# Folded x rounded to bf16 in one step, tables over all 256 features, weights loaded into freed buffers: what each part does to the time

## Chip, cores, metric

The kernel runs on one core of a Trainium2 chip. The metric is the time of one execution in microseconds of the device (us), as the median of several executions. "Ratio" always means the mean time of one kernel's fast runs over the mean time of the fast runs of the kernel before in the same rounds on the same chip, so it is not quite the ratio of the medians that are quoted beside it. A run that the record marks as slow (over 1.5% above the fastest of its kernel) is left out of the ratios. Engines: TensorE (PE in the profile, PEld its weight loads), VectorE (DVE), ScalarE (ACT), GpSimd (POOL), SyncE (SP).

## The reference

A Fourier mixing of x (8 x 2496 x 256, the real part of a transform over both axes) is followed by a mixture of 8 experts with balanced assignment: all (token, expert) logits are sorted, and each token goes to the first expert in that order which is not yet full.

```python
X = np.fft.fft(np.fft.fft(x, axis=1), axis=2).real        # (8, 2496, 256) -> 19968 tokens
logits = x @ w_gate                                        # 256 -> 8 experts
order = np.argsort(-logits.flatten())                      # greedy, capacity N // E per expert
for idx in order: ...                                      # first free expert wins
for e in range(E):
    out[assigned == e] = np.maximum(x[assigned == e] @ w1[e], 0) @ w2[e]   # 256 -> 1024 -> 256
```

The kernel does not sort the logits. It assigns most tokens in a first round ("early" tokens, 40 tiles), starts the experts on them, and settles the rest beside them ("settling": small VectorE steps with joins to TensorE). The tokens settled last form 16 "late" tiles, whose rows are gathered by index.

## The kernel before

Five stages follow each other: (1) fold x along both axes and project it on the gate, (2) logits, (3) first assignment, Fourier transforms, sorting of rows into expert tiles, (4) expert tiles with settling beside them, (5) the tail. The last cut is made in both kernels where tile 25 is put, that is, where its rows are scattered to the output by index: there the changed kernel gathers its first late rows, while the kernel before does so at tile 28. Names in the profiles: zt are transposed rows of x, hps and hb the hidden values of a tile before and after the ReLU, ops and ot its outputs, wps and w1t a turned w1, xg gathered late rows. The parts that the argument touches:

```python
# stage 1, per batch b of 8: fold to fp32 z, round z on ScalarE, transpose z
nc.vector.tensor_tensor(a_t[:, :, :, 1:D], a_t[:, :, :, 1:D], b_t[:, :, ::-1, D - 1:0:-1], op=AL.add)
nc.vector.tensor_tensor(a_t[:, :, :, 0], a_t[:, :, :, 0], b_t[:, :, ::-1, 0], op=AL.add)
z = early.tile([P, 2 * NK, D], FT, tag="z", bufs=2, name="z")
nc.vector.tensor_tensor(z[:, :, 1:P], pv[:, :, 1:P], pv[:, :, D - 1:P:-1], op=AL.add)
nc.vector.tensor_tensor(z[:, :, P + 1:D], pv[:, :, 1:P], pv[:, :, D - 1:P:-1], op=AL.subtract)
nc.scalar.copy(zball[:, b], z)
# ... transposes tp of z, copies zt <- tp on ScalarE, matmuls yps <- zt ...

# stage 3: one after the other
run(choose(True)); finish_round = raise_first(first_strips)      # assignment chain on VectorE
for n in range(4 * NT): transform(n)                             # TensorE
# ... four turn_w (w1 turned into the transformed basis), then the sorts ...

# stages 4 and 5: between parts of a tile, settling steps are taken from a generator
G0 = 28                                      # tile at which the first late gather is issued
def place_all():                             # whatever is left of the settling, at once
    if not placed: placed.append(len(list(todo)))
def pace():
    credit[0] = min(credit[0] + 1.4, 1.4)    # credit in us of VectorE work, per third of a tile
    while credit[0] > 0.0:
        c = next(todo, "end")
        if c is SYNC: return                 # a join: the rest waits for the next call
        credit[0] -= c
```

Of the kernel before, what the change touches and what calls it, by code (L numbers as in the profile page):

```python
# [8 lines left out]
FT = mybir.dt.float32  # L9
# [9 lines left out]
B = 8  # L19
S = 2496  # L20
# [33 lines left out]
KC = 64  # L54
SYNC = None
# [11 lines left out]
def kernel(  # L67
# [15 lines left out]

    tabs_cm = tc.tile_pool(name="tabs", bufs=1, side="right")
# [10 lines left out]
    for b in range(B):  # L95
        for i in range(NK):
            nc.gpsimd.iota(mir_i[:, b * NK + i:b * NK + i + 1], pattern=[[0, 1]],
                           base=(b + 1) * (S // 2) - 1 - (1 + i * P), channel_multiplier=-1)
    x_pairs = x.rearrange("b (s r) d -> (b s) (r d)", r=2)

    def load_x(b):
        a_t = early.tile([P, NK, 2, D], FT, tag="xa", bufs=2, name="xa")
        b_t = early.tile([P, NK, 2, D], FT, tag="xb", bufs=2, name="xb")
# [28 lines left out]
    kgrid_i = early.tile([P, KP], FT, tag="prod", bufs=1, name="kgrid_i").bitcast(I32)  # L132
# [60 lines left out]
    mt_f = early.tile([P, 2, D], FT, name="mt_f")  # L193
    mt_b = const.tile([P, 2, D], BF, name="mt_b")

    def phases(dst_r, kk, row, period):
        kw = dst_r.shape[-1]
        prod = early.tile([P, KP], FT, tag="prod", bufs=1, name="prod")[:, :kw]
        rnd = early.tile([P, KP], FT, tag="rnd", bufs=1, name="rnd")[:, :kw]
        nc.vector.tensor_scalar(prod, in0=kk, scalar1=row, scalar2=None, op0=AL.mult)  # L200
        nc.scalar.activation(rnd, prod, ACT.Copy, bias=0.0, scale=1.0 / period)
        nc.vector.tensor_scalar(rnd, in0=rnd, scalar1=MAGIC, scalar2=MAGIC, op0=AL.add, op1=AL.subtract)
        nc.vector.scalar_tensor_tensor(dst_r, in0=rnd, scalar=-float(period), in1=prod, op0=AL.mult, op1=AL.add)

    for dc in range(2):
        row = early.tile([P, 1], FT, tag="drow", bufs=2, name="drow")
        nc.vector.tensor_scalar(row, in0=iota_p, scalar1=float(dc * P), scalar2=None, op0=AL.add)
        r_t = early.tile([P, KP], FT, tag="rt", bufs=1, name="rt")[:, 0:P + 1]
        phases(r_t, kgrid[:, 0:P + 1], row, D)
        ra = early.tile([P, KP], FT, tag="ra", bufs=1, name="ra")[:, 0:P + 1]  # L210
        nc.vector.scalar_tensor_tensor(ra, in0=r_t, scalar=-1.0, in1=r_t, op0=AL.mult, op1=AL.max)
        nc.scalar.activation(mt_f[:, dc, 0:P + 1], ra, ACT.Sin, bias=halfpi, scale=-2.0 * PI / D)
        nc.scalar.activation(mt_f[:, dc, P + 1:D], r_t[:, 1:P], ACT.Sin, bias=0.0, scale=-2.0 * PI / D)
    nc.vector.tensor_copy(mt_b, mt_f)
# [3 lines left out]
    nc.vector.memset(g_sb, 0.0)  # L218
    gps = psl.tile([P, 512], FT, tag="tp", bufs=4, name="gps")
    for j in range(2):  # L220
        for dc in range(2):
            nc.tensor.matmul(gps[:, j * E:(j + 1) * E], lhsT=mt_f[:, dc, j * P:(j + 1) * P],
                             rhs=wg_sb[:, dc, :], start=(j == 0 and dc == 0), stop=(j == 1 and dc == 1))
    nc.vector.tensor_copy(g_sb[:, 0, 0:E], gps[:, 0:E])
    nc.vector.tensor_scalar(g_sb[:, 1, 0:E], in0=gps[:, E:2 * E], scalar1=is0, scalar2=None, op0=AL.mult)
    nc.vector.tensor_scalar(g_sb[:, 1, E:2 * E], in0=gps[:, E:2 * E], scalar1=not0, scalar2=None, op0=AL.mult)
# [5 lines left out]
    def gen_tab(i, r):  # L232
        period = S // 2 if r == 0 else S
        row = early.tile([P, 1], FT, tag="drow", bufs=2, name="drow")
        nc.vector.tensor_scalar(row, in0=m_cols[:, i:i + 1], scalar1=1.0 if r == 0 else 2.0,
                                scalar2=float(r), op0=AL.mult, op1=AL.add)
        r_t = early.tile([P, KP], FT, tag="rt", bufs=1, name="rt")
        phases(r_t, kgrid, row, period)
        ra = early.tile([P, KP], FT, tag="ra", bufs=1, name="ra")
        nc.vector.scalar_tensor_tensor(ra, in0=r_t, scalar=-1.0, in1=r_t, op0=AL.mult, op1=AL.max)  # L240
        n = "EO"[r]
        for nm, src, bias, scale in (("c" + n, ra, halfpi, -2.0 * PI / period), ("s" + n, r_t, 0.0, 2.0 * PI / period)):
            tf = early.tile([P, KP], FT, tag="tf", bufs=1, name="tf")
            nc.scalar.activation(tf, src, ACT.Sin, bias=bias, scale=scale)  # L244
            if i == NK - 1 and nm != "sE":
                nc.vector.tensor_scalar(tf, in0=tf, scalar1=own if nm == "cE" else skip, scalar2=None, op0=AL.mult)
            nc.scalar.copy(hi[nm][:, i, :], tf)
            nc.vector.tensor_tensor(lo[nm][:, i, :], tf, hi[nm][:, i, :], op=AL.subtract)


    zball = tabs.tile([P, B, 2 * NK, D], BF, name="zball")
# [6 lines left out]
    for b in range(B):  # L258
# [4 lines left out]
        z = early.tile([P, 2 * NK, D], FT, tag="z", bufs=2, name="z")  # L263
        nc.vector.tensor_tensor(z[:, :, 1:P], pv[:, :, 1:P], pv[:, :, D - 1:P:-1], op=AL.add)
        nc.vector.tensor_tensor(z[:, :, P + 1:D], pv[:, :, 1:P], pv[:, :, D - 1:P:-1], op=AL.subtract)
        nc.scalar.copy(z[:, :, 0:D:P], pv[:, :, 0:D:P])
        if b + 2 < B:
            load_x(b + 2)
        nc.scalar.copy(zball[:, b], z)  # L269


# [4 lines left out]
        for n0, nn in ((0, 4), (4, 4), (8, 2)):  # L276
            yps = psl.tile([P, 4, P], FT, tag="y", bufs=2, name="yps")
            for blk in range(2):
                tp = psl.tile([P, 4, P], FT, tag="tp", bufs=4, name="tp")
                for u in range(nn):  # L280
                    nc.tensor.transpose(tp[:, u, :], z[:, n0 + u, blk * P:(blk + 1) * P], identf)  # L281
                zt = early.tile([P, 4, P], FT, tag="zt", bufs=2, name="zt")
                nc.scalar.copy(zt[:, 0:nn, :], tp[:, 0:nn, :])  # L283
                nc.tensor.matmul(yps[pb:pb + 2 * E, 0:nn, :], lhsT=g_sb[:, blk, :], rhs=zt[:, 0:nn, :],  # L284
                                 start=(blk == 0), stop=(blk == 1))
            nc.scalar.copy(yt[pb:pb + 2 * E, n0:n0 + nn, :], yps[pb:pb + 2 * E, 0:nn, :])  # L286

        if b % 4 == 3:
            for n0, nn in ((0, 4), (4, 4), (8, 2)):
                ytp = psl.tile([P, 4, P], FT, tag="tp", bufs=4, name="ytp")  # L290
# [12 lines left out]
    ps_cm.__exit__(None, None, None)  # L303


    asg_c = ctx.enter_context(tc.tile_pool(name="asg_c", bufs=1, side="left"))
    lg = asg_c.tile([P, E, GC], FT, name="lg")
    with tc.tile_pool(name="pslog", bufs=1, space=PS) as pslog:
# [14 lines left out]
        pool6 = early.tile([P, 2 * NK, D], FT, tag="z", bufs=2, name="pool6").rearrange("p a d -> p (a d)")  # L323
        t6 = [pool6[:, q * 320:(q + 1) * 320].rearrange("p (k f) -> p k f", k=NK) for q in range(6)]
# [59 lines left out]
    mv = asg.tile([P, GC], FT, name="mv")  # L384
    mvv = mv.rearrange("p (b q k) -> p b q k", b=B, q=4)
    nc.gpsimd.memset(mv, -1.0e9)  # L386
    tail0 = asg.tile([P, 1], FT, name="tail0")
    tail1 = asg.tile([P, 1], FT, name="tail1")
    head1 = asg.tile([P, 1], FT, name="head1")
    nc.gpsimd.tensor_scalar(tail0, in0=iota_p, scalar1=113.0, scalar2=2.0e9, op0=AL.is_ge, op1=AL.mult)  # L390
    nc.gpsimd.tensor_scalar(tail1, in0=iota_p, scalar1=112.0, scalar2=2.0e9, op0=AL.is_ge, op1=AL.mult)
    nc.gpsimd.tensor_scalar(head1, in0=is0, scalar1=2.0e9, scalar2=None, op0=AL.mult)
    for q in range(4):
        nc.gpsimd.tensor_scalar(mvv[:, :, q, NK - 1], in0=mvv[:, :, q, NK - 1],
                                scalar1=tail0 if q < 2 else tail1, scalar2=None, op0=AL.add)
        if q % 2 == 1:
            nc.gpsimd.tensor_scalar(mvv[:, :, q, 0], in0=mvv[:, :, q, 0], scalar1=head1, scalar2=None, op0=AL.add)


    base = asg.tile([P, E, GC], BF, name="base")  # L400
    for e in range(E):
        nc.gpsimd.memset(base[:, e, :], float(2 * e * SEG))
# [16 lines left out]
    rampw_i = asg.tile([P, EW + 2], I32, name="rampw_i")  # L419
# [5 lines left out]

    def payloads():
        pay_i = rampw_i[:, 0:GC]
        nc.gpsimd.iota(rampw_i, pattern=[[1, EW + 2]], base=1, channel_multiplier=0)
        nc.gpsimd.tensor_copy(rampw, rampw_i)
        for q, (s1, s2) in enumerate(((0, 1), (2, -1), (1, -1), (1, 1))):  # L430
            for par in range(2):
                nc.gpsimd.iota(pay_i.rearrange("p (n k b q) -> p n k b q", n=4, k=NK, b=2)[:, :, :, par, q],
                               pattern=[[2 * S, 4], [s2 * P, NK]], base=PAY0 + S // 2 * s1 + par * S,
                               channel_multiplier=s2)
# [27 lines left out]
    def choose(first):  # L462
# [20 lines left out]
        for e in range(E):  # L483
            nc.scalar.activation(cjunk, dd[:, e, :], ACT.Relu, bias=1.0, scale=K_CNT, accum_out=cnt[:, e:e + 1])  # L484
            busy["A"] += 0.33
            if e % 4 == 3:
                yield 0.3
# [699 lines left out]
```

## Time and profile before

Three timed runs before the change: median 702.12 us (696.42 to 705.18). The profile of the kernel before that came with them spans only 658.9 us. First the page's line of busy times, then the view of busy time by stretch; each row of that is a stage.

```profile
PE 517.7 (79%) x4003; PEld 359.7 (55%) x4003; DVE 428.8 (65%) x1062; ACT 362.5 (55%) x842; POOL 318.1 (48%) x399
```

```profile
core 0: us, PE busy (x) PEld busy (x) DVE busy (x) ACT busy (x) POOL busy (x), PEclk, DMA share, GB/s
0.00:138.90 138.90, 81.70 (x285) 30.37 (x286) 92.04 (x167) 90.47 (x153) 59.12 (x88) 0.87 0.50 152
138.90:153.00 14.10, 12.96 (x316) 12.65 (x317) 8.75 (x15) 4.75 (x8) 0.00 (x0) 0.82 0.02 4
153.00:249.30 96.30, 67.65 (x536) 51.02 (x534) 63.16 (x155) 40.40 (x107) 39.80 (x93) 0.91 0.91 224
249.30:432.20 182.90, 169.99 (x1367) 124.12 (x1364) 140.89 (x418) 134.33 (x367) 77.45 (x74) 0.97 0.29 91
432.20:659.00 226.80, 185.38 (x1509) 141.54 (x1506) 123.98 (x309) 92.57 (x208) 141.69 (x145) 0.91 0.21 67
```

No engine is full in stage 1 and 3 (TensorE 82 of 139 and 68 of 96 us); in stage 4 TensorE is (170 of 183). In stage 1 the page's group of gate matmuls shows what TensorE waits for: 28.6 us idle before them, 28.4 of it for the ScalarE copies zt.

```profile
L284 PE MATMUL yps<-zt,g_sb 128*16 128x512 f32 (+1 forms) x96 | 50.7, 636 | 28.6 <-ACT zt L283 28.4
```

In the tail, the waits between 440 and 490 us (engine, line, what it waited for: us in all, times, longest) show a hole: the settling left over at tile 28 runs alone, while GpSimd waits 25.2 us for its result before it can gather, ScalarE 26.3 us for the next hidden matmul, and TensorE serves the chain in short bursts (19.26 us busy of the 40 from 440 to 480).

```profile
ACT hb L860 <- PE hps L1036: 27.7, 5, 26.3
POOL xg L1012 <- DVE wa L671: 25.2, 1, 25.2
PE inv_ps L649 <- DVE o_eq L645: 19.1, 8, 10.4
```

### The profile page before, as it was taken

The numbers are of one execution on the slowest core, as the hardware profiler recorded it, in microseconds if no ns is written. First come the engines' busy times: TensorE is split into PE (matmuls) and PEld (weight loads), VectorE is DVE, ScalarE is ACT, GpSimd is POOL, SyncE is SP. The second block draws the span as 40 slices with busy tenths as digits, with TensorE's granted clock in tenths as the row PEclk, the third lists the DMA queues.
The fourth block names the chain that finished last, engine by engine and source line by source line (L and its number), as shares of the span: only waits on it lengthen the run. The fifth ranks groups of instructions, "written<-read, shape, count | busy, mean of one in ns | idle before, by whom it ended". The sixth has DMA issues, their size and how long they took to land.

```text
span 658.9 us, 11484 instructions
## 1 busy us (share of the span) xinstructions
PE 517.7 (79%) x4003; PEld 359.7 (55%) x4003; DVE 428.8 (65%) x1062; ACT 362.5 (55%) x842; POOL 318.1 (48%) x399
## 2 busy tenths in 40 slices
PE   0675697666688659989979999894399999887894
PEld 0321232265467435657757777673377777665673
DVE  3887694368785457868858878768875555433451
ACT  1478776764145446767767867753055455333451
POOL 8786410006433411534524444433067777777774
PEclk9979867879789998999989999997589999989898
DMA  8778440003996784422222323221012222222221
GB/s 257 220 238 265 145 151 1 0 2 46 239 268 247 233 246 107 118 70 90 98 69 96 116 91 103 88 80 39 0 55 80 82 78 87 72 66 67 78 83 56
DMA packets 35169, 74.63 MB, mean 113 GB/s; under 512 B 6115, under 2 KB 14349, under 8 KB 35104
## 3 DMA queue, kind: packets, MB, share of 16 engines
q0 software_dynamic: 23296, 42.10, 24.5%
q1 hardware_dynamic: 11808, 31.73, 14.1%
q8 instruction: 33, 0.54, 0.4%
q14 instruction: 32, 0.26, 0.1%
HBM read 51.26 MB, written 32.24 MB: 127 GB/s over the span
## 4 chain that ended last, share of the span: by engine, by line
PE 55%; DVE 13%; ACT 12%; DMA 9%; POOL 5%; issue 4%; POOLq 0%; DVEq 0%; ACTq 0%; SPq 0%
PE hps L1036 18%; PE ops L1047 17%; PE yps L284 6%; PE fftps L882 3%; PE sps L960 3%; DMA out_dram<-ot,rows_l 3%; ACT zball L269 3%; ACT cjunk L484 2%; DMA t_dram<-stage 2%; PE tp L281 2%; POOL xg L1012 1%; DMA w1raw<-in_moe_w_dram 1%; ACT tf L244 1%; ACT yt L286 1%; DMA xl<-t_dram 1%
## 5 line engine op out<-in xcount | busy, mean ns | idle before, releaser
L1047 PE MATMUL ops<-w2t,hb 128*128 128x256 bf16 (+1 forms) x1344 | 177.6, 276 | 11.0 <-ACT ot L860 11.0
L1051 POOL DMA_INDIRECT out_dram<-ot,rid x120 | 124.2, 1035 | 121.1 <-ACT ot L860 78.0
L860 ACT ACTIVATE hb<-hps 128x384 bf16<-128x384 f32 (+1 forms) x293 | 131.1, 490 | 74.0 <-PE hps L1036 68.5
L1047 PEld LDWEIGHTS <-hb 128*128 128x128 bf16 (+1 forms) x1344 | 134.2, 100 | 46.3 <-issue 14.2
L1036 PE MATMUL hps<-xs,w1t 128*128 128x384 bf16 x640 | 132.2, 333 | 6.3 <-DVE xs L866 4.0
L1036 PEld LDWEIGHTS <-w1t 128*128 128x128 bf16 x896 | 87.0, 100 | 53.7 <-issue 15.1
L864 DVE TENSOR_SCALAR hb<-hps 128x384 bf16<-128x384 f32 (+1 forms) x155 | 82.3, 546 | 50.4 <-PE hps L1036 37.6
L860 ACT ACTIVATE ot<-ops 128x256 f32<-128x256 f32 x111 | 42.5, 383 | 87.8 <-PE ops L1047 44.0
L284 PE MATMUL yps<-zt,g_sb 128*16 128x512 f32 (+1 forms) x96 | 50.7, 636 | 28.6 <-ACT zt L283 28.4
L1012 POOL DMA_INDIRECT xg<-t_dram,ids_l x48 | 46.4, 966 | 39.5 <-DVE wa L671 25.2
L866 DVE COPY ot<-ops 128x256 f32<-128x256 f32 (+1 forms) x57 | 24.2, 424 | 61.8 <-PE ops L1047 32.0
L113 POOL DMA_INDIRECT xb<-in_x_dram,mir_i x40 | 52.9, 1321 | 20.9 <-issue 14.1
L1051 POOL DMA_INDIRECT out_dram<-ot,rows_l x48 | 47.1, 982 | 16.1 <-issue 7.0
L1036 PE MATMUL hps<-xt,w1t 128*128 128x384 bf16 (+1 forms) x256 | 49.7, 328 | 0.0
L960 PE MATMUL sps<-pt,xl 128*128 128x192 bf16 x320 | 33.5, 248 | 4.3 <-DMA xl<-t_dram 2.7
L281 PEld LDWEIGHTS tp<-identf,z 128*128 128x128 f32 x160 | 20.5, 163 | 28.2 <-issue 22.7
L860 ACT ACTIVATE xs<-sps 128x384 bf16<-128x384 f32 x65 | 28.7, 489 | 11.9 <-PE sps L960 11.8
L892 POOL COPY stage<-stage 128x258 bf16<-128x258 bf16 x40 | 17.3, 443 | 34.5 <-DVE stage L888 30.5
L891 ACT ACTIVATE stage<-stage 128x254 bf16<-128x254 bf16 x40 | 16.5, 415 | 30.0 <-DVE stage L888 27.4
L284 PEld LDWEIGHTS yps<-zt,g_sb 128*16 128x16 f32 x96 | 6.4, 100 | 48.4 <-ACT zt L283 41.3
L386 POOL MEMSET mv<- 128x160 f32 x1 | 0.2, 231 | 67.2 <-PE fftps L882 67.2
L960 PEld LDWEIGHTS <-xl 128*128 128x128 bf16 x320 | 28.0, 99 | 7.0 <-DMA xl<-t_dram 2.9
(326 smaller groups left out, 834.8 us busy)
## 6 DMA issues: line engine op xcount, KB each, us to landing
t_dram<-stage SPq DMA_DIRECT2D x20, 512.0 KB
xl<-t_dram SPq DMA_DIRECT2D x20, 512.0 KB
xa<-in_x_dram SPq DMA_DIRECT2D x8, 1024.0 KB
w1raw<-in_moe_w_dram POOLq DMA_DIRECT2D x8, 512.0 KB, 8.2
w2t<-in_moe_w_dram POOLq DMA_DIRECT2D x8, 512.0 KB, 17.0
out_dram<-ot,rid POOLq DMA_INDIRECT x120, 2.5
xa<-in_x_dram SPq DMA_DIRECT2D x8, 224.0 KB
xg<-t_dram,ids_l POOLq DMA_INDIRECT x48, 2.6
```

The source lines that it names most:

```text
L113: nc.gpsimd.indirect_dma_start(out=bv[0:n, i, :], out_offset=None, in_=x_pairs, in_offset=bass.IndirectOffsetOnAxis(ap=mir_i[0:n, b * NK + ...
L269: nc.scalar.copy(zball[:, b], z)
L281: nc.tensor.transpose(tp[:, u, :], z[:, n0 + u, blk * P:(blk + 1) * P], identf)
L284: nc.tensor.matmul(yps[pb:pb + 2 * E, 0:nn, :], lhsT=g_sb[:, blk, :], rhs=zt[:, 0:nn, :], start=(blk == 0), stop=(blk == 1))
L860: nc.scalar.activation(dst, src, ACT.Relu if relu else ACT.Copy)
L864: nc.vector.tensor_scalar(dst, in0=src, scalar1=0.0, scalar2=None, op0=AL.max)
L866: nc.vector.tensor_copy(dst, src)
L960: nc.tensor.matmul(sps[:, j2 * EW:(j2 + 1) * EW], lhsT=xl[:, 2 * g + cc, j2 * P:(j2 + 1) * P], rhs=pt[:, 2 * g + cc, 0:EW], start=(cc == 0 ...
L1012: nc.gpsimd.indirect_dma_start(out=xg[0:nr, q, :], out_offset=None, in_=t_dram, in_offset=bass.IndirectOffsetOnAxis(ap=d["ids"](q, nr), ax ...
L1036: nc.tensor.matmul(hps[:, 0:n], lhsT=w1t[d["e"]][:, j2, fc * P:(fc + 1) * P], rhs=d["x"](j2), start=(j2 == 0), stop=(j2 == 1))
L1047: nc.tensor.matmul(ops[0:nr, 0:D], lhsT=d["hid"][:, fc, b0:b0 + nr], rhs=w2t[d["e"]][:, fc, :], start=(fc == 0), stop=(fc == F // P - 1))
L1051: put = nc.gpsimd.indirect_dma_start(out=out, out_offset=bass.IndirectOffsetOnAxis(ap=d["rows"](b0 // P)[0:nr], axis=0), in_=ot[0:nr, :], ...
```

## The change

The intent: take ScalarE and VectorE work out of stage 1, load weights where the DMA queues idle (DMA share 0.00 from 100 to 140 us before), overlap the assignment chain with the transforms, and have the settling done when the first late gather is due. The core of the diff, with cuts:

```diff
 # stage 1
-        z = early.tile([P, 2 * NK, D], FT, tag="z", bufs=2, name="z")
-        nc.vector.tensor_tensor(z[:, :, 1:P], pv[:, :, 1:P], pv[:, :, D - 1:P:-1], op=AL.add)
-        nc.vector.tensor_tensor(z[:, :, P + 1:D], pv[:, :, 1:P], pv[:, :, D - 1:P:-1], op=AL.subtract)
-        nc.scalar.copy(zball[:, b], z)
+        zb = zball[:, b]                       # bf16 directly; transposes now read pv, not z
+        nc.vector.tensor_tensor(zb[:, :, 1:P], pv[:, :, 1:P], pv[:, :, D - 1:P:-1], op=AL.add)
+        nc.vector.tensor_tensor(zb[:, :, P + 1:D], pv[:, :, 1:P], pv[:, :, D - 1:P:-1], op=AL.subtract)
+    # gate table over all 256 features (8 matmuls instead of 4); zt copies of both halves merged;
+    # x buffers xa 3 deep, in a pool of their own that is freed after stage 1
-        nc.scalar.activation(rnd, prod, ACT.Copy, bias=0.0, scale=1.0 / period)      # phases
+        nc.vector.tensor_scalar(n1, in0=kgrid[:, 0:w], scalar1=turns, scalar2=MAGIC, op0=AL.mult, op1=AL.add)
+        ...
+        nc.scalar.activation(ra, r_t, ACT.Abs)         # was a VectorE operation
 ...
 # after stage 1: two w1 and all w2 loaded into the freed space; w1 of e+2 after turn_w(e)
 # stage 3: the chain is a generator; half-transforms are put between its steps by a modelled clock
+    for c in first_chain():
+        if c is not SYNC:
+            clock["D"] += c
+            while clock["PE"] < clock["D"] - 1.0 and unit(): pass
+            continue
+        ...
+    for n in range(4):
+        sort_mark(n); unit(); sort_call(n, (0, 1)); unit(); sort_call(n, (2, 3)); reload(n + 3)
+    sort_rows(0, 0)
+    while unit(): pass
+    while pending: pending.pop(0)()            # last combine: VectorE joins the halves of a transform
 # stage 4 and 5
-        credit[0] = min(credit[0] + 1.4, 1.4)
+        credit[0] = min(credit[0] + 1.9, 1.9)
-    for e in range(4, E): at(e - 3, 0, lambda e=e: turn_w(e))
+    for e in range(1, E): at(e - 1, 1, lambda e=e: turn_w(e))     # 7 turns beside tiles, was 4
-    G0 = 28
+    G0 = 25                                    # all late gathers spaced 1.5 tiles (was: the first 8)
+    # output ring widened from 8 to 18 tiles once the settling is done
```

## The prediction

> **What bounds the kernel now.** The page: span 658.9 us; PE 79% busy, DVE 65%, ACT 55%, POOL 48%. The timed runs are slower (median 702.12); the profile does not say why. The timeline by stage shows different limits.
>
> 1. 0 to 138 us, folding x and projecting the gates: no engine full (20-us windows: PE 11 to 19, DVE 8 to 18, ACT 14 to 16 busy). By the waits, PE loses 28.4 us to the zt copies, which queue on ACT behind 2.33-us zball casts and table work. x has landed by about 97 us; the rest is backlog.
> 2. 138 to 152 us: logits, PE bound.
> 3. 152 to 249 us: first assignment, then transforms, then four w1 turns. PE idles during the assignment (4.15 of 10 us busy at 170 to 180), POOL builds constants first (153.7 to 167), and the late weight loads hold PE (a 9.09-us piece of the chain).
> 4. 249 to 450 us: 28 expert tiles, 7 us each; PE 93% busy, DVE 77%, ACT 73%.
> 5. 450 to 659 us: POOL waits 25.2 us for the decode and PE loses 21 us at 440 to 480 (the build dumps 20.4 us of modelled DVE work at tile 28). From 484 us POOL issues one indirect DMA every 1.28 us without a break: 135 of them, 173 us. The ot copies wait about 57 us for scatters.
>
> **What the change does, costed.**
> - Stage 1: removes the zball cast (2.33 x 8) and rnd (0.72 x 10) from ACT, adds Abs (about 0.72 x 10), merges zt copies, removes ra from DVE (0.82 x 10). Transposes need only the first fold, and the instruction order keeps a batch's matmuls together. ACT comes to about 77 us, DVE 93, x load 90. Estimate: ends near 108 instead of 138, a gain of 25 to 30.
> - Stage 3: PE needs 43 us for transforms, 6 for sorting, 2 for one turn; DVE about 58. Interleaved: about 65 instead of 97. Weights load while DMA was idle (100 to 160). Gain 30 to 35.
> - Experts: settling is nearly done by tile 25 (4.6 us left), but denser: modelled DVE plus ACT rises from 282 to 323 us over 25 tiles. I expect 190 us for them, against 184 now: no gain.
> - Tail: from tile 25 POOL has 141 indirect DMAs, 181 us at 1.28; PE needs 32 tiles of about 5.6 us, 180. Wider gather spacing and 18 output buffers let both run together; the stall at 450 to 484 goes. Gain about 30.
>
> All gains but the expert part are on the critical path; the profile should show about 108+13+5+65+190+185 = 566 us. [...]
>
> Scaled by 702/660, the timed median is about 604 us, range 574 to 636. Chances: faster 0.96, within 2% 0.03, slower 0.01.
>
> **Signs.** Right: first logits matmul by 115; first hps before 195; no POOL wait above 10 us near the decode; POOL at one DMA per 1.28 us to the end. Wrong: tiles above 8 us in the first 25 (DVE and ACT the limit); turns waiting for w1raw, now loaded only two tiles ahead; xb gathers limiting stage 1.
>
> **What would make it wrong.** Interleaved PE and DVE queues stalling each other[...]; the denser pace costing the tiles more than 190 us; timed runs slowed by something the profile hides.

What the profile of before shows: the granted clock is 0.50 from 460 to 480 us, where TensorE is busy for 7.43 us of 20, and 1.00 from 380 to 400, where it is busy for 19.03. The 43 us for the transforms are an estimate; stage 3 of this profile has 46.4 us of them (busy TensorE).

## The result

After the change the median is 663.31 us (four runs, 659.43 to 668.24), before it 701.9 in the same rounds; the ratio is 0.9461 (95% interval 0.9373 to 0.955). That is clearly faster, but outside the predicted range of 574 to 636 us. The profile of the changed kernel (668.24 us, span 666.4), by stage, columns as above:

```profile
0.00:124.80 124.80, 75.24 (x294) 37.21 (x295) 91.23 (x156) 73.68 (x126) 86.64 (x75) 0.90 0.58 175
124.80:139.00 14.20, 11.24 (x318) 10.56 (x319) 4.26 (x10) 1.04 (x3) 2.56 (x4) 1.00 1.42 199
139.00:220.30 81.30, 60.73 (x510) 48.37 (x510) 58.91 (x151) 36.27 (x91) 24.30 (x62) 0.89 0.63 196
220.30:432.50 212.20, 193.15 (x1506) 137.38 (x1512) 169.43 (x516) 149.38 (x390) 86.70 (x84) 0.95 0.33 93
432.50:666.00 233.50, 182.87 (x1383) 134.67 (x1381) 92.51 (x203) 87.32 (x188) 135.42 (x139) 0.91 0.19 61
```

These rows must not be set against those of before: as the experiments show, the two profiles are of different speed in the tail. The gain and the chip are separated in the first experiment.

Two things can be read at once. ScalarE has 73.7 us of work in stage 1 instead of 90.5. And the tail of this profile holds waits that the profile of before does not have, on something "remote", in a program of one core:

```profile
DVE hb L886 <- remote: 15.1, 6, 5.2
ACT hb L882 <- remote: 10.9, 3, 6.0
DVE ot L888 <- remote: 7.5, 2, 3.8
```

One such place, in the timelines of TensorE, ScalarE and VectorE (start, us, engine, line, operation, [idle before <- what ended it]):

```profile
507.26 0.81 PE L1103 MATMUL hps<-xs,w1t 128*128 128x384 bf16 x4
513.27 0.80 PE L1103 MATMUL hps<-xs,w1t 128*128 128x384 bf16 x2 [5.20 <-issue]
```

```profile
513.39 0.49 ACT L882 ACTIVATE hb<-hps 128x384 bf16<-128x384 f32 x1 [6.00 <-remote]
```

```profile
511.23 0.42 DVE L888 COPY dd<-ops 128x256 f32<-128x256 f32 x1 [5.22 <-remote]
```

TensorE starts nothing for 5.20 us, and both readers of its results stand still as long. The matmuls shown as finished by 508.1 reported late. The next semaphore updates of TensorE that the trace records stand at 511.20, 512.63 and 513.37, each just before a reader starts (VectorE at 511.23 and 512.66, ScalarE at 513.39). "Remote" is here only the profile's word for a release that it can match to no instruction that ended just before; "issue" is time for which it shows no wait. So for these matmuls the shown end and the release of the readers lie 3 us and more apart (508.1 against 511.20). Gaps of 2.5 to 5.2 us before a hidden matmul stand at 442.97, 459.65, 489.55, 513.27, 535.77, 555.76, 580.23 and 604.42, that is every 17 to 30 us, all between the issue of the first late gather (427.06) and that of the last (605.47).

### The profile page after: what moved, and what is told of

It reads as the page before. It is cut to its first block, busy times and chain, and to the rows that moved or that the text cites. A ratio compares the mean times of both kernels' runs of the same rounds, so it can differ in the third digit from the quotient of the medians.

```text
span 666.4 us, 11324 instructions
## 1 busy us (share of the span) xinstructions
PE 523.2 (79%) x4003; PEld 368.2 (55%) x4011; DVE 416.3 (62%) x1033; ACT 347.7 (52%) x797; POOL 335.6 (50%) x360
## 4 chain that ended last, share of the span: by engine, by line
PE 36%; issue 10%; DVE 9%; POOL 7%; ACT 3%; another core or an unknown queue 2%; DMA 0%; POOLq 0%; DVEq 0%; ACTq 0%
PE hps L1103 16%; PE ops L1126 14%; POOL out_dram L1130 5%; PE sps L974 3%; ACT cjunk L496 2%; PE wps L939 1%; POOL xs L1079 1%; DVE pt L952 1%; ACT hb L882 1%; DVE wa L480 1%; DVE dd L493 1%; DVE wa L484 1%; PE rp L1001 1%; PE inv_ps L657 1%
## 5 line engine op out<-in xcount | busy, mean ns | idle before, releaser
L1130 POOL DMA_INDIRECT out_dram<-ot,rid x95 | 100.5, 1058 | 131.0 <-ACT ot L882 94.2
L116 POOL DMA_INDIRECT xb<-in_x_dram,mir_i x40 | 65.1, 1628 | 15.9 <-issue 10.5
L304 PE MATMUL yps<-zt,g_sb 128*16 128x512 f32 (+1 forms) x96 | 41.8, 566 | 23.5 <-ACT zt L302 23.3
L882 ACT ACTIVATE ot<-ops 128x256 f32<-128x256 f32 (+1 forms) x86 | 33.0, 384 | 44.8 <-PE ops L1126 24.6
L300 PE MATMUL tp<-identf,xa 128*128 128x128 f32 x160 | 27.7, 337 | 13.4 <-DVE xa L283 6.7
L300 PEld LDWEIGHTS tp<-identf,xa 128*128 128x128 f32 x160 | 23.7, 177 | 23.9 <-issue 16.3
L888 DVE COPY ot<-ops 128x256 f32<-128x256 f32 (+1 forms) x32 | 13.6, 424 | 36.5 <-PE ops L1126 14.7
L1130 POOL DMA_INDIRECT out_dram<-ot,rows_l x23 | 22.3, 968 | 18.8 <-ACT ot L882 7.9
L952 DVE TENSOR_SCALAR pt<-rampw,spot 128x193 bf16<-128x193 bf16 x160 | 31.2, 287 | 0.2 <-PE inv_ps L657 0.2
L282 DVE TENSOR_TENSOR xa<-xa,xb 128x2550 f32<-128x2550 f32 x8 | 22.5, 2816 | 13.9 <-DMA xb<-in_x_dram,mir_i 7.9
```

The lines of the kernel that those rows point to most:

```text
L116: nc.gpsimd.indirect_dma_start(out=bv[0:n, i, :], out_offset=None, in_=x_pairs, in_offset=bass.IndirectOffsetOnAxis(ap=mir_i[0:n, b * NK + ...
L300: nc.tensor.transpose(tp[:, blk, u, :], pv[:, n0 + u, blk * P:(blk + 1) * P], identf)
L304: nc.tensor.matmul(yps[pb:pb + 2 * E, 0:nn, :], lhsT=g_sb[:, blk, :], rhs=zt[:, blk, 0:nn, :], start=(blk == 0), stop=(blk == 1))
L882: nc.scalar.activation(dst, src, ACT.Relu if relu else ACT.Copy)
L952: nc.vector.tensor_scalar(marks[n][:, f, 0:EW + 1], in0=rampw[:, 0:EW + 1], scalar1=spot[:, c:c + 1], scalar2=None, op0=AL.is_equal)
L1130: put = nc.gpsimd.indirect_dma_start(out=out, out_offset=bass.IndirectOffsetOnAxis(ap=d["rows"](b0 // P)[0:nr], axis=0), in_=ot[0:nr, :], ...
```

## The experiments

Eighteen kernels ran, in five jobs; within a job all run on one chip with the kernel before. The jobs' medians of before:

| job | chip | before, us | its kernels |
|---|---|---|---|
| 1 | 9 | 658.07 | a_again, a_zero, b_again, b_zero |
| 2 | 10 | 699.50 | a_pace14, b_pace19, a_noring, a_flush |
| 3 | 0 | 699.91 | a_third, a_fold, a_serial, a_combo |
| 4 | 15 | 697.12 | a_cast, a_phases, a_tabs2, b_third |
| 5 | 10 | 700.09 | a_zero2, a_best |

Labels with a_ are edits of the changed kernel, with b_ of the kernel before. So kernels of different jobs are compared by their ratio to before, and by stages of their profiles.

### Two chips, two speeds: a_again, b_again, a_zero, b_zero

a_again and b_again are the two kernels unchanged. The zero variants make the hidden values zero (the result is wrong), to see whether the late completions depend on the values:

```diff
-            nc.scalar.activation(dst, src, ACT.Relu if relu else ACT.Copy)
+            nc.scalar.activation(dst, src, ACT.Relu if relu else ACT.Copy, bias=0.0, scale=0.0 if zero else 1.0)
-                take(w1t[e][:, j, fs], wps)
+                take(w1t[e][:, j, fs], wps, zero=True)
```

(On VectorE the same copy becomes a multiplication by zero.)

> The kernel before, unchanged, for a profile beside its own timed runs. Open question: its first profile has 660.7 us, its four timed runs 696 to 705. Theory A (slow episodes of TensorE): beyond the granted clock that the trace lists, TensorE sometimes completes matmuls 2 to 6 us late; the profile after shows about 8 such episodes (waits put down to remote, 54 us in sum over engines), the first profile of before none. Then this profile is near 700 and shows such waits, and the extra 40 us lie where they are. Theory B (profiling or chip): this profile is near 660 again while the timed runs stay at 700, or all runs are at 660 on this chip, without remote waits.

> The changed kernel, unchanged, on the same chip as b_again: ratio 0.93 to 0.96 as before under both theories. Theory A: remote waits on TensorE again, in the tail from 440 us on, 20 to 40 us in sum of PE idle time. Theory B: their number is unrelated to the time.

> The changed kernel with w1t multiplied by 0 as it leaves PSUM, so that the expert matmuls work on zeros (output wrong on purpose, routing and instruction stream as before). Theory A[...]: they are gone, 20 to 35 us less than a_again (ratio to before about 0.90). Rival C (instruction supply, semaphores or scheduling): within 1% of a_again, episodes as before.

> The kernel before with w1t multiplied by 0 in the same way (output wrong on purpose). Theory A: about 660 instead of 700 (ratio 0.94), no remote waits. Rival C: ratio 0.99 to 1.01.

Measured: b_again 659.48 us, ratio 1.0075 (0.994 to 1.021); a_again 609.94, ratio 0.9318 (0.9213 to 0.9422); a_zero 612.77, 0.9351 (0.925 to 0.945); b_zero 659.0, 1.0053 (0.995 to 1.016). Zeros change nothing. (Two of the seven runs of before were slow, and the record calls all four verdicts of this job unclear.) But this chip is faster for both kernels, and no wait on "remote" is in any of the four profiles. The stages of b_again and then of a_again:

```profile
0.00:137.30 137.30, 79.52 (x285) 30.42 (x285) 92.61 (x167) 90.41 (x153) 59.37 (x88) 0.88 0.49 153
137.30:151.50 14.20, 13.06 (x318) 12.72 (x319) 8.95 (x15) 4.76 (x8) 0.00 (x0) 0.83 0.01 4
151.50:246.40 94.90, 67.53 (x535) 50.82 (x534) 62.98 (x155) 40.42 (x107) 39.78 (x93) 0.91 0.92 228
246.40:432.20 185.80, 172.74 (x1407) 126.53 (x1406) 144.43 (x423) 136.71 (x375) 79.07 (x77) 0.99 0.30 94
432.20:653.00 220.80, 179.94 (x1466) 137.80 (x1463) 120.64 (x304) 89.56 (x200) 139.68 (x142) 0.91 0.21 65
```

```profile
0.00:119.80 119.80, 75.93 (x292) 38.65 (x292) 91.06 (x156) 73.76 (x126) 80.16 (x75) 0.91 0.62 183
119.80:134.00 14.20, 12.21 (x313) 11.61 (x314) 4.07 (x8) 0.85 (x2) 2.48 (x3) 0.88 1.42 198
134.00:213.70 79.70, 59.86 (x516) 47.90 (x513) 59.12 (x153) 36.06 (x91) 24.31 (x62) 0.91 0.63 200
213.70:425.90 212.20, 192.82 (x1518) 136.92 (x1516) 169.30 (x515) 150.21 (x393) 86.61 (x83) 0.96 0.33 93
425.90:607.40 181.50, 164.75 (x1380) 128.03 (x1378) 93.28 (x203) 87.08 (x185) 135.64 (x139) 0.97 0.25 78
```

This is the balance of the change on one chip: stage 1 gains 17.5 us, the logits nothing, stage 3 15.2, the 25 tiles lose 26.4, the tail gains 39.3; together 45.6. GpSimd now waits 2.9 us for the late index, not 25:

```profile
POOL xg L1079 <- DVE wa L679: 2.9, 1, 2.9
```

The balance also shows where the chips differ: against the changed kernel's first profile (124.8, 14.2, 81.3, 212.2, 233.5) the tiles take exactly as long, and 52 of the 59 us lie in the tail.

### What the slower chips lose: b_third, a_zero2

b_third is the kernel before, unchanged, for a profile on a slower chip. a_zero2 is a_zero again, because on chip 9 nothing is late that zeros could mend. (Its theory is that the late completions depend on the values.)

> The kernel before, unchanged, for its profile on this chip. If the chip is one of the slow ones (about 700): the same times as on the other chip up to tile 25 (put at about 432), late matmul completions and waits on remote only after about 450, and a tail of about 265 instead of 221 us. Rival: the slowness is spread over all stages in proportion (tile 25 at about 460).

> The changed kernel with the turned w1 scaled by zero, so that all hidden values are zero (wrong on purpose), once more, because the first time it ran on the one fast chip, where nothing is late. If this chip is a slow one (before about 700): theory '[...]': the late completions after tile 25 go away or shrink, and the whole falls from about 664 towards 620. Rival 'they depend on how dense the matmuls come, or on the chip, not on the data': within 6 us of 664. On a fast chip it tells nothing (about 612).

Measured: b_third 696.65 us. Its tail row, to be set against the 220.80 of b_again:

```profile
435.30:695.00 259.70, 191.78 (x1466) 141.56 (x1464) 120.88 (x304) 90.44 (x200) 139.75 (x142) 0.87 0.18 56
```

Tile 25 is put at 435.3 us (432.2 on chip 9), as the first expectation said, and the tail is 39 us longer; TensorE shows only 12 us more busy time for it, the rest is idle. a_zero2 took 664.09 us (its profile fell in the slow state), ratio 0.9494 (0.9459 to 0.9529), as the changed kernel on such chips (664.9 in a_third, in another job). So the values of the turned w1, and the hidden values that follow from them, are not the cause; x and w2 were not zeroed. The granted clock is 1.00 or 0.50 and nothing between in the traces of before and after (17 and 18 stretches of 0.50), and 0.91 on average over the tail of b_again, 0.87 over that of b_third; whether it has a part in the late completions was not shown.

What the runs do show is where the gaps of over 2 us lie: after the first late gather and until the last one (gathers at 427 to 605 us and gaps at 443 to 604 in the first profile of after; at 476 to 636 and 512 to 641 in b_third, whose last gap begins just after the last gather has been issued). So they go with that phase of the program, not with a time since its start. A later run makes the tie closer. From 480 us on, each gap in the first profile of after overlaps every second group of three gathers, the last one 600.8 to 604.4 with the gathers that start at 602.9 to 605.5. In a_best, whose gathers begin three tiles later, a gap again overlaps the last gathers (599.5 to 603.0, with 601.5 to 604.0), three tiles further in the program than the last gap of a_flush. So the gaps move with the gathers and do not belong to a place among the tiles. That they are caused by the gathers is not shown: chip 9 runs the same gathers without one such gap (b_again has three of 2.2 to 2.3 us, before output matmuls that wait for ScalarE), and why the other chips have them stays open.

Two rivals stand untested. "Chip" is here all that differs between jobs, as only chip 10 ran in two. And the traces differ in what they hold: those of chip 9 and the first one of before have 8,368 to 8,539 records of semaphore updates, all others 5,804 to 6,091, with nearly the same number of instructions (11,321 to 11,484). Every run, the timed ones too, has a span and a clock that were recorded, so that the recording itself delays TensorE on those chips is not excluded. Slower transfers are not what the traces show: from 480 to 600 us a packet of the gathers' queue took 114 and 121 ns on average in a_again and b_again, 117 and 123 in the first profile of after and in b_third (120 in the first of before).

### The pace of the settling: a_pace14, b_pace19

```diff
 # a_pace14                                                  # b_pace19: the reverse, in the kernel before
-        credit[0] = min(credit[0] + 1.9, 1.9)
+        credit[0] = min(credit[0] + 1.4, 1.4)
```

> The changed kernel with the pace credit of the settling chain set back from 1.9 to 1.4. Built this way, 44 of its steps (29.1 us by the kernel's own cost figures, 10 of them joins) are left when the first late gather needs them at tile 25; in the changed kernel 5 steps (4.55 us) are left. Theory 'the denser pace pays': the 25 tiles get shorter by about 10 us (212 to 202), a stall of 30 to 45 us appears at tile 25, and the whole is about 630 us (620 to 640; ratio to before near 0.96) where the unchanged after had 610 on an undisturbed chip. Rival 'the denser pace is what lost 25 us in the tiles': tiles back to about 190, stall about 25, the whole within 5 us of 610.

> The kernel before with only the pace credit set from 1.4 to 1.9. Built this way nothing of the settling chain is left at tile 28 (before: 33 steps, 20.4 us by its own figures, and a stall of 34 us between tile 28 at 444.8 and the next put at 479). Theory 'the tail gain is mainly the pace': the stall goes, the tiles take some 8 to 12 us more, the whole 658 to about 633 us (ratio 0.95 to 0.97). Rival 'the settling work only changes its place': the whole within 8 us of before (ratio 0.99 to 1.0).

Measured: a_pace14 672.57 us, ratio 0.9615 (0.957 to 0.966), where the changed kernel has 0.9502 (a_third, below). Split at tile 24, tile 25 and the end, first a_pace14, then a_noring of the same job, whose pace is 1.9:

```profile
213.80:394.60 180.80, 172.33 (x1378) 124.19 (x1382) 145.79 (x424) 134.77 (x355) 79.44 (x78) 0.99 0.36 104
394.60:435.20 40.60, 14.23 (x119) 11.07 (x118) 36.70 (x123) 4.20 (x10) 5.88 (x6) 0.62 0.08 25
435.20:670.00 234.80, 186.97 (x1396) 136.71 (x1394) 91.57 (x197) 86.64 (x189) 135.49 (x139) 0.89 0.19 61
```

```profile
218.00:418.40 200.40, 182.29 (x1417) 128.88 (x1425) 159.59 (x481) 143.52 (x377) 80.38 (x78) 0.96 0.32 94
418.40:430.20 11.80, 10.19 (x93) 8.10 (x91) 9.73 (x35) 6.33 (x15) 6.33 (x6) 1.00 0.27 84
430.20:664.00 233.80, 179.12 (x1380) 132.51 (x1378) 91.50 (x203) 85.40 (x186) 135.89 (x139) 0.94 0.19 61
```

This is the clearest pair. With the low credit, 24 tiles take 180.8 us, nearly the 179 of before (246.4 to 425.3 in b_again), although three more turns of w1 run beside them. With 1.9 they take 200.4. In return the step to tile 25 takes 11.8 us instead of 40.6, of which GpSimd waits 30.1 for the late index:

```profile
POOL xg L1079 <- DVE wa L679: 30.1, 1, 30.1
```

After tile 25 both take the same 234 us. So the denser pace itself costs 20 us in the tiles and saves 29. Of the 20, half is busy time of TensorE (172.3 to 182.3 us) and half its idle time (8.5 to 18.1); through which wait the pace does this was not isolated. Both theories had one half right.

b_pace19 shows the same trade in the kernel before: 687.64 us, ratio 0.9835 (0.979 to 0.9881, so unclear at the 2% mark), a gain of about 12 us where 25 were expected. Below, b_pace19 split at the put of tile 28; then b_again, with the stall of before in a row of its own:

```profile
249.60:471.40 221.80, 202.54 (x1637) 148.10 (x1640) 175.44 (x535) 158.85 (x431) 94.74 (x89) 0.96 0.27 85
471.40:686.00 214.60, 167.07 (x1232) 120.72 (x1230) 80.15 (x169) 75.69 (x166) 127.69 (x130) 0.88 0.19 61
```

```profile
246.40:444.80 198.40, 185.34 (x1508) 136.05 (x1507) 154.44 (x453) 146.01 (x398) 85.31 (x82) 0.99 0.29 92
444.80:479.00 34.20, 13.58 (x115) 11.13 (x114) 29.84 (x103) 5.00 (x13) 6.11 (x7) 0.60 0.07 21
479.00:653.00 174.00, 153.75 (x1252) 117.13 (x1249) 80.78 (x172) 75.25 (x166) 127.33 (x130) 0.96 0.24 74
```

From the first expert matmul to tile 28 before needs 198.4 + 34.2 = 232.6 us, b_pace19 221.8: 11 us saved, not the whole stall. (The last rows are not comparable, as b_pace19 ran on a slower chip.)

### The output ring: a_noring

```diff
-            ring["more"] += [v[:, D * i:D * (i + 1)] for i in range(5)]
+            pass
```

> The changed kernel without the ten more output tiles (ring of 8 throughout). Theory 'the wider ring matters in the tail': waits on the way out appear before the output evictions after tile 25, the tail grows from 181 to about 190, the whole about 618 us. Rival 'the tail's rate is set by TensorE and at the end by the scatter issues on GpSimd, 1.28 us each': within 3 us of 610.

Measured: 665.49 us, ratio 0.95 (0.9459 to 0.9541), tail 233.8 us: the same as with the ring, so the rival holds, on a slower chip. On chip 9, where the tail has no gaps, it was not tried.

### Stage 3: a_serial, a_flush, a_third

a_third is the changed kernel, unchanged, as a yardstick. a_serial takes the interleave away; a_flush keeps it and only emits the last combine earlier:

```diff
 # a_flush (a_serial has this too)
+    while unit(): pass
+    while pending: pending.pop(0)()
     for n in range(4):
         sort_mark(n)
-        unit()
         sort_call(n, (0, 1))
-        unit()
         ...
     sort_rows(0, 0)
-    while unit(): pass
-    while pending: pending.pop(0)()
 # a_serial, besides
-    for c in first_chain(): ...   (half-transforms between the steps)
+    for c in first_chain(): pass
```

> The changed kernel, unchanged, as the yardstick of this job, since the chips differ (before 658 and after 610 on one, before 700 and after about 663 on the two others). Theory: 610 or 663, ratio to before 0.93 to 0.95; first logits matmul at 120 to 125, first expert matmul at 213 to 220.

> The changed kernel with the interleave undone: the whole first assignment chain, then all transforms, then the sorts (with the last combine before the sorts as in a_flush). Theory 'the interleave is what shortened stage 3': from the end of the logits to the first expert matmul about 95 us as in before, instead of 80, and the whole 12 to 20 us longer than the unchanged one of this job. Rival 'the early weights and the constants built during stage 1 gave the gain': 75 to 82 us, the whole within 5 us.

> The changed kernel with the last transform combine and its store emitted before the first sorts instead of behind them (today the last combine runs at 206.7, behind the first sort's row tables, and ScalarE then waits 2.93 us for that store before the first weight eviction at 211.4). Theory 'this order costs the hole at 206 to 213': first expert matmul at about 208 instead of 213.7 and the whole about 604 us (ratio about 0.92). Rival 'the tiles after it are set by something else': first expert matmul earlier but the whole within 2 us of 610.

Measured: a_third 664.9 us, ratio 0.9502 (0.945 to 0.9553); a_serial 672.03, 0.9595 (0.9549 to 0.9641); a_flush 655.89, 0.9393 (0.9338 to 0.9448). Stage 3 (end of the logits to the first expert matmul) in a_third, a_serial and a_flush:

```profile
140.70:221.10 80.40, 59.51 (x511) 47.50 (x510) 59.06 (x152) 36.13 (x91) 24.38 (x62) 0.91 0.64 198
```

```profile
136.00:226.80 90.80, 63.13 (x525) 52.00 (x527) 62.45 (x152) 35.55 (x91) 23.71 (x62) 0.81 0.56 176
```

```profile
136.50:209.70 73.20, 56.87 (x509) 46.32 (x508) 59.52 (x151) 35.57 (x91) 24.56 (x62) 0.95 0.68 217
```

a_serial and a_flush differ by the interleave alone: it is worth 17.6 us. Without it stage 3 takes 90.8 us, near the 94.9 of before, so the rest of the change in this stage (early weights and constants, three of the four turns moved beside the tiles) gave about 4 in sum. And the changed kernel threw 7 us of the gain away. VectorE runs the first sort's row tables before the last combine, in a_again (two pieces of its timeline):

```profile
205.87 0.95 DVE L991 TENSOR_TENSOR bt<-rampw,spot_hi 128x768 bf16<-128x768 bf16 x1
206.74 0.68 DVE L919 TENSOR_TENSOR stage<-ev,fftps 128x512 bf16<-128x512 f32 x1
```

```profile
211.40 2.29 ACT L882 ACTIVATE w1t<-wps 128x512 bf16<-128x512 f32 x4 [2.93 <-DMA t_dram<-stage]
```

The store of that combine must land before w1t may take over its buffer, so ScalarE waits 2.93 us and TensorE behind it. In a_flush the same evictions come right after the sorts:

```profile
207.13 2.06 ACT L882 ACTIVATE w1t<-wps 128x512 bf16<-128x512 f32 x4 [0.42 <-PE sps L974]
```

So in a_again the combine, whose matmuls had ended at 184 us, ran only at 206.7, after the row tables, where the program emits it. The first profile of after shows that VectorE did not take it earlier: the combine's matmuls end at 189.3 us and its ScalarE copy at 188.9, it runs at 213.3, and in between VectorE stands idle for 1.06 and 2.44 us (until 205.03 and 210.92), waiting for matmuls of the sort.

### Stage 1: a_cast, a_phases, a_fold, a_tabs2

a_cast writes the fold in fp32 again and rounds it on ScalarE. a_phases restores the phases and the absolute value of before. a_fold exchanges the two instructions of the first fold. a_tabs2 makes the tables two batches earlier.

```diff
 # a_cast
+        z = early.tile([P, 2 * NK, D], FT, tag="z", bufs=1, name="z")     # both folds write z
+        nc.scalar.copy(zb, z)
 # a_phases: prod on VectorE, ACT.Copy to rnd, rounding and ra on VectorE, as in before
 # a_fold
+        nc.vector.tensor_tensor(a_t[:, :, :, 0], ...)        # narrow one first
         nc.vector.tensor_tensor(a_t[:, :, :, 1:D], ...)
-        nc.vector.tensor_tensor(a_t[:, :, :, 0], ...)
 # a_tabs2
-    tab_plan = [tab_order[0:2], tab_order[2:4]] + [[t] for t in tab_order[4:10]] + [[]]
+    tab_plan = [tab_order[0:4], tab_order[4:6]] + [[t] for t in tab_order[6:10]] + [[], [], []]
```

> The changed kernel with the second fold written in fp32 again and rounded by a ScalarE copy per batch (2.33 us, 8 times), all else as changed. Theory 'never keeping fp32 is the main gain of stage 1': first logits matmul 10 to 15 us later than in the unchanged one (120 to 126), so at 132 to 140, and the whole about 12 us longer (675 where unchanged has 664; 622 where it has 610). Rival 'the merged zt copies and the transposes taken from the first fold gave it, ScalarE has room': within 4 us.

> The changed kernel with the phases as before (product on VectorE, scaling on ScalarE, rounding on VectorE, absolute value on VectorE): one more VectorE operation per table (0.5 to 0.8 us, 10 times), as many on ScalarE. Theory 'busy time of VectorE carries through': first logits matmul about 6 us later. Rival 'slack elsewhere hides it': within 3 us of the unchanged one, which itself varies by 3.

> The changed kernel with the two instructions of the first fold exchanged: the narrow one (column 0, 0.18 us) first, the wide one (2.81 us) after it. In the changed kernel's trace the last batch's wide fold ends at 99.3, but its narrow one runs only at 106.7, behind table work that waits for ScalarE, and TensorE waits 7.1 us for it. Theory 'queue order on VectorE held stage 1': first logits matmul 5 to 8 us earlier than in the unchanged one of this job (about 113 instead of 120), the whole 5 to 8 us less. Rival 'stage 1 is limited by ScalarE's and VectorE's busy time, or by the loads': within 2 us.

> The changed kernel with the ten cosine and sine tables made two batches earlier (four before the first batch, two after it, one after each of the next four, none in the last three) instead of two, two and six single ones. Theory '[...]': first logits matmul at 112 to 118, the whole 5 to 8 us less. Rival 'the sum of the work sets the end': within 3 us.

(a_tabs2's theory is that in the last batches VectorE, ScalarE and TensorE wait for each other through the table work.)

Measured: a_cast 677.73 us, ratio 0.9707 (0.9652 to 0.9762); a_phases 674.17, 0.9653 (0.9589 to 0.9716); a_fold 659.94, 0.9441 (0.9393 to 0.9488); a_tabs2 664.22, 0.9538 (0.9474 to 0.9602). Stage 1 of a_third, a_cast and a_phases:

```profile
0.00:126.60 126.60, 77.16 (x293) 37.28 (x294) 91.22 (x156) 73.71 (x126) 84.03 (x75) 0.92 0.58 173
```

```profile
0.00:141.70 141.70, 84.09 (x292) 34.54 (x292) 89.83 (x156) 89.89 (x134) 78.74 (x75) 0.84 0.50 154
```

```profile
0.00:137.20 137.20, 77.75 (x293) 37.09 (x293) 98.01 (x168) 74.25 (x126) 85.73 (x77) 0.86 0.56 163
```

a_cast adds 16.2 us of ScalarE work and ends stage 1 15 us later; a_phases adds 6.8 us of VectorE work and ends it 11 us later. (a_third is the slowest of the ten profiles with this stage unaltered, 119.8 to 126.6 us, so both delays may be up to 7 us more. And a_phases also puts a ScalarE step back into the middle of a chain on VectorE, so it does not measure added work alone.) Neither engine is full (90 of 142, 98 of 137), yet the added work comes through whole or more. Each undoing alone gives back the whole gain of 17.5 us or most of it, so the two parts are not shares of one sum: the engines pass every batch round in a ring (fold, transposes, zt copy, matmul, yt copy), and each part of the ring waits for another (this is read from the waits, no run tests it alone: in a_again, from 15 to 118 us, the gate matmuls wait 18.4 us for zt, yt 20.5 for the gate matmuls, zt 5.5 for the transposes, the transposes 7.1 for the fold and the fold 3.5 for the transposes). The scatter of stage 1 between unchanged builds is not small (119.8 to 126.6 us in the profiles with this part unaltered), so single microseconds should not be read from it.

Of the two repairs neither is shown to work. The expectation of a_fold had misread the trace. The wait of 7.1 us for the narrow fold stands at the first batch, not at the last, and there a_fold shortens it by 1.7 us (a_again, then a_fold):

```profile
21.16 3.68 PE L300 MATMUL tp<-identf,xa 128*128 128x128 f32 x16 [7.08 <-DVE xa L283]
```

```profile
19.43 3.68 PE L300 MATMUL tp<-identf,xa 128*128 128x128 f32 x16 [5.34 <-DVE xa L283]
```

The last batch's transposes stand in both kernels behind a matmul that waits for zt: they start at 107.02 us in a_again and at 108.59 in a_fold, although the fold was complete at 102.4 there. Stage 1 ended at 123.0 us, inside the scatter, and the interval overlaps that of a_third (by time it is 5 us less). It is inconclusive. a_tabs2 ended stage 1 at 127.0, so its theory fell. What sets the end of stage 1 beyond the ring as a whole stays open.

### Together: a_combo, a_best

a_combo is a_fold and a_flush together. a_best is a_flush with credit 1.7 and G0 = 28.

> The changed kernel with both mends: narrow fold first, and the last combine before the first sorts. If both are on the critical path and independent, their gains add: 12 to 15 us less than the unchanged one (about 597 where that has 610, about 650 where that has 663). If the first only lets the second's wait grow, 7 to 8 us less.

> The changed kernel with the last combine before the first sorts (as a_flush), pace credit 1.7 and the first late gather at tile 28 (built this way one settling step is left there). Theory 'density itself costs, by queueing between VectorE and TensorE': the tiles per us rise, and the whole is 4 to 8 us below a_flush, ratio to before about 0.93. Rival 'the settling work costs its sum wherever it is spread': within 3 us of a_flush (ratio about 0.94), 28 tiles ending at about the same time as in a_flush.

Measured: a_combo 655.54 us, ratio 0.9344 (0.9292 to 0.9396), 9 us less than a_third in the same job; a_best 657.89, 0.9403 (0.9351 to 0.9456). a_combo is what a_flush gives, with perhaps 3 us from the fold (the intervals overlap). In a_best tile 28 is put at 431.5 us instead of 443.5, but from there to the end it takes 226 us instead of 210, and the late gathers begin three tiles later: nothing is won in all, as the rival said. The version to keep is a_flush (or a_combo): about 7 to 9 us below the changed kernel.

## Why the prediction was wrong, point by point

The prediction said "about 108+13+5+65+190+185 = 566 us", and "scaled by 702/660" 604. On chip 9 the same sum is 119.8 + 14.2 + 79.7 + 212.2 + 181.5 = 607.4: of the 41 us too many, 12 lie in stage 1, 10 in stage 3, 22 in the tiles, and the tail has 3.5 less. In the scored profile the sum is 666, and there the tail misses most, by 48.5 us.

- "Ends near 108 instead of 138": stage 1 ended at 119.8 to 126.6. The work that it said would go did go (ScalarE 73.7 us, it said about 77; VectorE 91, it said 93). The failed step is the jump from these busy times to an end 15 us above the largest of them. a_cast and a_phases show that in this ring added work comes through to the end even though no engine is full. Gain 17.5 us, not 25 to 30.
- "Interleaved: about 65 instead of 97" (70 with the 5 us of logits handling): 79.7. The mechanism was right, and a_serial and a_flush put it at 17.6 us. The size was off by 10 us; 7 of them are the last combine, queued behind the row tables (a_flush). That queues would stall each other was named as a danger; which one was not seen.
- "I expect 190 us for them, against 184 now: no gain": 212.2. On chip 9 this was the largest mis-sized term. The prediction saw the modelled VectorE and ScalarE work rise from 282 to 323 us over 25 tiles, and booked the 30 us that this saves in the tail, but next to nothing for the tiles. a_pace14 measures both sides: 20 us lost in 24 tiles, 29 saved at tile 25. Its own sign, tiles above 8 us (8.5 on average), came true, and so did its second danger, "the denser pace costing the tiles more than 190 us".
- "181 us at 1.28 [...] the stall at 450 to 484 goes. Gain about 30": right, 181.5 us and 39 gained on chip 9. The GpSimd wait at the decode fell from 25 us to 2.9. For the gathers and scatters of the tail, of up to 128 rows, a_again shows GpSimd instructions of 0.96 to 1.06 us on average (spans on GpSimd are rough), with 0.30 us before the next, 1.28 us from start to start, without a break for most of the tail on chip 9: a row of them can fill GpSimd. The ring of 18, to which the prediction gave part of the credit, was worth nothing measurable on a slower chip (a_noring). In the scored profile the tail took 233.5 us, and the sign "one DMA per 1.28 us to the end" failed.
- "Scaled by 702/660": this mixed two speeds. The profile of before came from a run of 660 us, its timed runs took 702; b_third shows that the difference is not a factor on every stage: 39 of its 42 us lie in the tail. The changed kernel loses 52 us there; why more than the kernel before is not shown. The prediction's last danger ("timed runs slowed by something the profile hides") was this. The factor also hid part of the error by luck: it added 38 us to every sum, where the slower chips add 52 to the tail. With 607.4 for 566 the ratio on chip 9 of 0.93 would have been right; scaled it would have been 646, still short of 663.

## What to carry to other kernels

When deferred work is moved from a stall into busy stages, book it on both sides: here 29 us saved cost 20, and both are read from the same two rows of a profile. A stage in which several engines hand batches round need not end with its fullest engine (here 90 us of 142 in a_cast); take one piece of work out or put one in, and see what comes through. Before scaling a profile to timed runs, find out in which stage the two differ, by a second profile from the slower runs.
